# A chain of expert steps: scattered ids in buffers of their own, the weight split in wide pieces on ScalarE and VectorE alone, results scaled on ScalarE

## The chip, the cores and the metric

The kernel runs on one core of one Trainium2 chip. The metric is the device time of one execution in microseconds. Three runs of the kernel before took 517.78, 515.27 and 517.69 us, median 517.69. TensorE multiplies matrices, VectorE (DVE) and ScalarE (ACT) work element by element and can read PSUM, GpSimd (POOL) issues the indirect DMAs and can do elementwise work on SBUF, SyncE (SP) issues the other DMAs.

## The reference, cut to what matters

Three stages follow each other: a linear attention with decay over 2 x 768 tokens, a dense feed-forward block with layer norm, and a mixture of experts with sticky routing. The change touches the last stage alone:

```python
def _moe2_ref(x, w_gate, w_local, w1, w2):
    ...
    for b in range(B):
        prev_e = -1
        for s in range(S):
            fresh_e = int(np.argmax(logits[b, s]))
            if s == 0 or local_gate[b, s] < 0.5:
                e = fresh_e
            else:
                e = prev_e if prev_e >= 0 else fresh_e
            prev_e = e
            ...
            h = np.maximum(x[b, s] @ w1[e], 0.0)
            out[b, s] = p[e] * (h @ w2[e])
```

There are 8 experts, x has 384 columns, w1 is 384 x 1024 and w2 1024 x 384 per expert.

## The kernel before

All matmuls that need fp32 accuracy are made of products of two halves: a value is split into a high half (ScalarE writes it rounded, L143) and a low half (the rest, written by VectorE or POOL, L148), and three products are summed: high with high, high with low, low with high. Weights are split as well as activations.

The program up to about 318 us (attention, dense block, routing, and the first 256 rows of the fullest expert) is one list of tasks written out by hand (`ORDER`). Behind it stands the chain of expert steps, in an order that is also written by hand (`manual_schedule`). Each engine runs its instructions in the order in which the code issues them.

`step(e, t, before, o)` (L990) does the first half of tile t of expert e (128 rows each) and the second half of the tile that came before it:

- If t > 0, TensorE transposes the gathered rows of this tile (`xpose_pe`), and after the result (below) they are split into `xq` (`xpose_split`).
- The tile before: `turn_pe` transposes its hidden values `hs` (8 transposes), `result(o)` (L985) multiplies the finished output of the tile before that, which stands in PSUM bank 4, by its gate value `cur_p` into the buffer `o`, and POOL scatters `o` to the output rows `cur_i` by an indirect DMA. `turn_split` splits the transposed hidden values into `H`.
- `first` (L953) multiplies this tile by w1 in two halves of 512 columns, 9 matmuls each, and ScalarE writes each half through a Relu to `hs`.
- `second(before)` (L976) multiplies `H` by w2 into bank 4, 24 matmuls.
- In a step with t = 0 and e > 0 the weights are filled: w2 of this expert (needed in the next step's `second`) and w1 of the next expert. `fill` (L178) splits one piece of 512 columns; there are six of w2 (numbers 6 to 11) and six of w1 (0 to 5). `fl(0)` and `fl(1)` issue two and three pieces behind the two halves of `first`, `fl(2)` the rest behind `second`. `POOL_C` names four of the twelve pieces whose low half POOL writes; VectorE writes the others. The rows of the next expert's first tile are transposed and split in the same step, and POOL gathers rows for later tiles (`get`).
- `load_a`, `load_b` load raw weights for later experts on SP's queue.
- `shift` (L946) moves the ids and gate values along on VectorE with four copies: `cur_i`, `cur_p` get the next tile's, and `nxt_i`, `nxt_p` this tile's. The copy to `cur_i` has to wait until the scatter that reads `cur_i` is over.

`others(e, t)` (L1030) wraps every further tile of an expert into `tc.If` on the expert's count of rows; the steps for t = 1 to 11 are nested, so an expert with few rows jumps over the rest. At a jump each engine adds what it left out to its semaphore, so that others wait for it to be past the If. Which steps run depends on the data; with these inputs, by the trace, experts 2 and 4 have two further tiles, 5 and 6 have one, 0, 1, 3 and 7 have none.

The outputs go to `XR[t % 2]` for t > 0 and to `XH[e % 2]` for t = 0; `cur_i` and `cur_p` are one column each of two small tiles (`now`).

Of the kernel before, what the change touches and what calls it, by code (L numbers as in the profile page):

```python
# [14 lines left out]
I32 = mybir.dt.int32  # L15
ACTF = mybir.ActivationFunctionType
ALU = mybir.AluOpType
# [5 lines left out]
DM = NH * HD  # L23
# [3 lines left out]
NE, EF = 8, 1024  # L27
# [8 lines left out]
C_ID, C_MK, C_RV, C_FT, C_JT, C_IO, C_TI, C_EO, C_JH, C_NC = 0, 128, 192, 200, 204, 220, 348, 360, 361, 385  # L36
HMAX = 2 * JMAX
POOL_LO = (7, 9, 11)
POOL_C = (7, 9, 11, 2)


SEQ = [(0, 0), (0, 1), (0, 2), (0, 3), (1, 0), (0, 4), (0, 5), (1, 1), (1, 2), (1, 3), (1, 4), (1, 5)]
# [59 lines left out]
def moe_kernel(ctx: ExitStack, tc: tile.TileContext, rT, kT, rn, kn, vn, wt, un, gt, w_c, wg, w1, w2,  # L102
               cst, cst_b, out, dbg=None):
    nc = tc.nc
    PE, DVE, ACT, POOL, SP = nc.tensor, nc.vector, nc.scalar, nc.gpsimd, nc.sync
# [8 lines left out]
    B = [BB[:, i] for i in range(8)]  # L114
# [15 lines left out]
    XH = [const.tile([128, DM], F32, name=f"xh{i}") for i in range(2)]  # L130
# [11 lines left out]
    def split(dst_hi, dst_lo, src, relu=False, lo_eng=None):  # L142
        ACT.activation(out=dst_hi, in_=src, func=ACTF.Relu if relu else ACTF.Copy)  # L143
        if relu:
            DVE.scalar_tensor_tensor(out=dst_lo, in0=src, scalar=0.0, in1=dst_hi.bitcast(F32),
                                     op0=ALU.max, op1=ALU.subtract)
        else:
            (lo_eng or DVE).tensor_tensor(out=dst_lo, in0=src, in1=dst_hi.bitcast(F32), op=ALU.subtract)  # L148


    raws, sets = [], []

    XR = []

    def raw_set(pool, i):
        return pool.tile([128, KD, EF], F32, name=f"wa{i}"), pool.tile([128, KE, DM], F32, name=f"wb{i}")

    def split_set(pool, i):
        return tuple(pool.tile(s, F32R, name=f"{n}{i}") for n, s in (
            ("w1h", [128, KD, EF]), ("w1l", [128, KD, EF]), ("w2h", [128, KE, DM]), ("w2l", [128, KE, DM])))  # L160

    def load_a(e):
        if e < NE:
            for n in range(2):
                s = slice(n * 512, n * 512 + 512)
                SP.dma_start(out=raws[e % 2][0][:, :, s], in_=r3(w1[e], KD)[:, :, s])
# [11 lines left out]
    def fill(e, i, pool=POOL_LO):  # L178
        fill_set(raws[e % 2], sets[(e + 1) % 2], i, pool)

    def fill_set(raw, ws, i, pool=POOL_LO):
        a, c = raw
        w1h, w1l, w2h, w2l = ws
        if i < 6:
            k, n = i % 3, i // 3
            ns = slice(n * 512, n * 512 + 512)
            hi, lo, src = w1h[:, k, ns], w1l[:, k, ns], a[:, k, ns]
        else:
            n = slice((i - 6) * 512, (i - 5) * 512)
            hi, lo, src = (t.rearrange("p k f -> p (k f)")[:, n] for t in (w2h, w2l, c))  # L190
        split(hi, lo, src, lo_eng=POOL if i in pool else DVE)

    def gather(dst, off, n=NTOK):
        POOL.indirect_dma_start(dst, None, xd[0:n, :], IndirectOffsetOnAxis(ap=off, axis=0),
                                bounds_check=n - 1, oob_is_err=False)

    def xpose_pe(x, i):
        px = r3(B[6 + i][:, 0:DM], KD)
        for k in range(KD):
            PE.transpose(px[:, k, :], x[:, k * 128:(k + 1) * 128], ident)  # L200

    def xpose_split(i):
        s = slice(i * 128, i * 128 + 128)
        split(XQ[:, 0, :, s], XQ[:, 1, :, s], r3(B[6 + i][:, 0:DM], KD))

    if True:
# [496 lines left out]
        def load_top():  # L703
            a, c = raws[0]
            for t, w_ in ((a, w1), (c, w2)):
                POOL.indirect_dma_start(t.rearrange("p k f -> p (k f)"), None, w_.rearrange("e p f -> (e p) f"),
                                        IndirectOffsetOnAxis(ap=top_w, axis=0), bounds_check=128 * NE - 1, oob_is_err=False)
# [50 lines left out]

        now = []

        def load_early():
            ast.close()
            rst = ctx.enter_context(tc.tile_pool(name="cr", bufs=1, side="right", reuse_waits="tile"))
            raws.append(raw_set(rst, 0))
            sets.append(split_set(rst, 0))
            hs_.append(rst.tile([128, EF], F32, name="hs"))
            XE[0] = rst.tile([128, 2, DM], F32, name="xe0")
            load_top()
# [9 lines left out]
        def fill0(i):  # L778
            fill_set(raws[0], sets[0], i)
# [122 lines left out]
        def close():  # L902
            bst.close()
            cl = ctx.enter_context(tc.tile_pool(name="cl", bufs=1, reuse_waits="tile"))
            sets.append(split_set(cl, 1))
            raws.append(raw_set(cl, 1))
            XR.extend(x2)
            XP[1] = cl.tile([128, 2, DM], F32, name="xp1")
            now.extend(cl.tile([128, 2], t, name=f"now_{n}") for n, t in (("i", I32), ("p", F32)))

        def zX(i):
            POOL.memset((XE[0], XP[1])[i], 0.0)

        def rows(e, t):

            return XP[e % 2][:, t % 2] if t else XE[e % 2][:, 0]

        def get(e, t):
            if e < NE and t < JMAX:
                gather(rows(e, t), ids[:, e, t:t + 1])  # L920
# [13 lines left out]
        with tc.manual_schedule():  # L934
            for t in ORDER.split():
                name, *a = t.split(".")
                name, _, e = name.partition(":")
# [15 lines left out]
        def first(e, i, fl):  # L953

            w1h, w1l = sets[(e + 1) % 2][:2]
            xh, xl = XT[0]
            t = slice(128 * i, 128 * i + 128)
            for n in range(2):
                ns = slice(n * 512, n * 512 + 512)
                todo = [(a_, w_, k) for k in range(KD) for a_, w_ in ((xh, w1h), (xh, w1l))] + [(xl, w1h, k) for k in range(KD)]  # L960
                for q, (a_, w_, k) in enumerate(todo):
                    PE.matmul(out=B[n], lhsT=a_[:, k, t], rhs=w_[:, k, ns], start=(q == 0), stop=(q == 8))  # L962
                ACT.activation(out=hs[:, ns], in_=B[n], func=ACTF.Relu)  # L963
                fl(n)

        def turn_pe(n):
            pt = r3(B[2 + n], 4)
            for k in range(4):
                f = 4 * n + k
                PE.transpose(pt[:, k, :], hs[:, f * 128:(f + 1) * 128], ident)  # L970

        def turn_split(n):
            f = slice(4 * n, 4 * n + 4)
            split(hh[:, f, 0:128], hl[:, f, 0:128], r3(B[2 + n], 4))
# [7 lines left out]
                        PE.matmul(out=B[4][:, 0:DM], lhsT=a_[:, k, 0:128], rhs=w_[:, k, :], start=(q == 0), stop=(q == 23))  # L982
                        q += 1

        def result(o):  # L985
            DVE.tensor_scalar(out=o, in0=B[4][:, 0:DM], scalar1=cur_p, scalar2=None, op0=ALU.mult)  # L986
            POOL.indirect_dma_start(out[:, :], IndirectOffsetOnAxis(ap=cur_i, axis=0), o[:, :], None,  # L987
                                    bounds_check=NTOK - 1, oob_is_err=False)

        def step(e, t, before, o):  # L990

            if t:
                xpose_pe(rows(e, t), 1)
            if before is not None:
                for n in range(2):
                    turn_pe(n)
                result(o)
            if t:
                xpose_split(1)
                get(e, t + 1)  # L1000
            if before is not None:
                for n in range(2):
                    turn_split(n)

            todo = [] if t or e == 0 else [(e, q) for q in range(6, 12)] + [(e + 1, q) for q in range(6) if e + 1 < NE]
            parts = todo[:2], todo[2:5], todo[5:]

            def fl(n):
                for q in parts[n]:
                    fill(*q, POOL_C)  # L1010

            first(e, int(t > 0), fl)
            if t == 0 and e + 1 < NE:
                xpose_pe(rows(e + 1, 0), 0)
                xpose_split(0)
                get(e + 2, 0)
                get(e + 1, 1)
            if before is not None:

                if t + 1 < JMAX:  # L1020
                    tc.mark_branch_hint_location(f"end{e}.{t + 1}", nts[e] > 2 * t + 2, engines=[PE.engine])
                second(before)
            fl(2)
            if t == 0:
                load_a(e + 3)
                if e:
                    load_b(e + 2)
            shift(e, t)

        def others(e, t):  # L1030
            if t < JMAX:
                with tc.If(nts[e] > 2 * t, label=f"end{e}.{t}"):  # L1032
                    step(e, t, e, XR[t % 2])
                    others(e, t + 1)

        ctx.enter_context(tc.manual_schedule())
# [1 line left out]
        DVE.memset(now[1], 0.0)  # L1038
        ld_n(0)
        for e in range(NE):  # L1040
            step(e, 0, e - 1 if e else None, XH[e % 2])
            if e + 1 < NE:
                ld_n(e + 1)
            others(e, 1)
        for n in range(2):
            turn_pe(n)
        result(XH[0])
        for n in range(2):
            turn_split(n)
        second(NE - 1)  # L1050
        shift(None, 0)
        result(XH[1])


def layout(inputs):
# [70 lines left out]
```

## Time and profile before

| | |
|---|---|
| median of three runs | 517.69 us |
| the profiled execution | 517.72 us |
| its span, first to last instruction | 515.9 us |
| mean granted TensorE clock | 0.934 |
| TensorE busy | 405.6 us (79%) |
| VectorE busy | 333.3 us (65%) |
| ScalarE busy | 184.0 us (36%) |
| POOL busy | 223.3 us (43%) |

The span is shorter than the time by what lies around the first and the last instruction. In a profile, a row of a timeline gives the start, the duration, the engine, the source line, the operation, what it writes and reads, the shapes, how many like instructions were merged into the row, and in brackets how long the engine idled before it and what ended that. A source line can be that of a helper, as L143 and L148 here: there the tile names tell which split it is. The letter q behind an engine (DVEq) stands for its sequencer, which waits, branches and issues.

### The profile page before, as it was taken

The numbers are of one execution on the slowest core, as the hardware profiler recorded it, in microseconds if no ns is written. First come the engines' busy times: TensorE is split into PE (matmuls) and PEld (weight loads), VectorE is DVE, ScalarE is ACT, GpSimd is POOL, SyncE is SP. The second block draws the span as 40 slices with busy tenths as digits, with TensorE's granted clock in tenths as the row PEclk, the third lists the DMA queues.
The fourth block names the chain that finished last, engine by engine and source line by source line (L and its number), as shares of the span: only waits on it lengthen the run. The fifth ranks groups of instructions, "written<-read, shape, count | busy, mean of one in ns | idle before, by whom it ended". The sixth has DMA issues, their size and how long they took to land. (4 is left out here: it accounts for less than half of the span.)

```text
span 515.9 us, 8879 instructions
## 1 busy us (share of the span) xinstructions
PE 405.6 (79%) x3297; PEld 366.9 (71%) x3297; DVE 333.3 (65%) x685; ACT 184.0 (36%) x471; POOL 223.3 (43%) x212
## 2 busy tenths in 40 slices
PE   2447586999899799999999793596891979879675
PEld 2336575998799799889988673485881767768564
DVE  7998999758647857775785981736244543736341
ACT  1463453314135122212432541653251612707040
POOL 6879879264325412713041251635133432615141
PEclk9999799999899899999999996878996889989897
DMA  8863371051033050003309556075306270310000
GB/s 256 281 199 138 119 269 34 21 186 32 2 104 104 15 159 3 32 1 143 136 0 339 213 175 269 23 258 177 122 18 214 85 248 32 98 66 15 9 20 15
DMA packets 24848, 59.69 MB, mean 116 GB/s; under 512 B 3994, under 2 KB 10598, under 8 KB 24512
## 3 DMA queue, kind: packets, MB, share of 16 engines
q1 hardware_dynamic: 21856, 50.85, 29.0%
q0 software_dynamic: 2912, 7.88, 4.3%
q8 instruction: 38, 0.62, 0.5%
q14 instruction: 42, 0.34, 0.2%
HBM read 56.35 MB, written 5.70 MB: 120 GB/s over the span
## 5 line engine op out<-in xcount | busy, mean ns | idle before, releaser
L506 PE MATMUL banks<-wh,H 128*128 128x384 f32 x288 | 84.9, 356 | 7.6 <-DVE H L494 6.5
L962 PE MATMUL banks<-w1h,xq 128*128 128x512 f32 x168 | 64.6, 456 | 18.8 <-DVE xq L148 14.3
L148 POOL TENSOR_TENSOR w2l<-wb,w2h 128x512 fp32r<-128x512 f32 x27 | 35.0, 1304 | 63.2 <-ACT w2h L143 63.1
L506 PEld LDWEIGHTS banks<-wh,H 128*128 128x128 f32 x288 | 54.7, 196 | 9.8 <-DVE H L494 7.5
L962 PEld LDWEIGHTS banks<-w1h,xq 128*128 128x128 f32 x168 | 36.7, 221 | 30.0 <-DVE xq L148 16.0
L491 ACT ACTIVATE H<-banks 128x512 fp32r<-128x512 f32 x36 | 21.3, 594 | 80.3 <-PE banks L487 73.6
L506 PE MATMUL banks<-wl,H 128*128 128x384 f32 x144 | 49.9, 347 | 0.0
L982 PE MATMUL banks<-w2h,H 128*128 128x384 f32 x224 | 47.1, 343 | 0.0
L148 DVE TENSOR_TENSOR w1l<-wa,w1h 128x512 fp32r<-128x512 f32 x48 | 46.7, 1028 | 0.1
L487 PE MATMUL banks<-xq,wh 128*128 128x256 f32 x216 | 43.8, 301 | 0.4 <-DVE xq L470 0.4
L148 DVE TENSOR_TENSOR w2l<-wb,w2h 128x512 fp32r<-128x512 f32 x27 | 23.4, 868 | 30.4 <-ACT w2h L143 30.4
L970 PE MATMUL banks<-cs,hs 128*128 128x128 f32 x112 | 18.2, 317 | 29.1 <-DVEq L1032 21.0
L982 PEld LDWEIGHTS banks<-w2h,H 128*128 128x128 f32 x224 | 39.8, 192 | 1.0 <-ACT H L143 0.3
L963 ACT ACTIVATE hs<-banks 128x512 f32<-128x512 f32 x28 | 16.8, 598 | 58.5 <-PE banks L962 58.5
L970 PEld LDWEIGHTS banks<-cs,hs 128*128 128x128 f32 x112 | 15.1, 164 | 31.5 <-issue 31.5
L962 PE MATMUL banks<-w1l,xq 128*128 128x512 f32 x84 | 37.1, 441 | 0.0
L487 PEld LDWEIGHTS banks<-xq,wh 128*128 128x128 f32 x216 | 35.9, 202 | 1.1 <-DVE xq L470 0.6
L494 DVE SCALAR_TENSOR_TENSOR H<-banks,H 128x512 fp32r<-128x512 f32 x36 | 24.5, 684 | 18.7 <-ACT H L491 18.6
L987 POOL DMA_INDIRECT out<-xh,now_i x9 | 9.1, 1006 | 58.5 <-DVE xh L986 52.5
L143 ACT ACTIVATE H<-banks 128x512 fp32r<-128x512 f32 x28 | 15.6, 597 | 48.9 <-PE banks L970 48.9
L986 DVE TENSOR_SCALAR xh<-banks,now_p 128x384 f32<-128x384 f32 x9 | 5.6, 618 | 42.4 <-PEq L1032 22.1
L487 PE MATMUL banks<-xq,wl 128*128 128x256 f32 x108 | 31.9, 295 | 0.6 <-DVE wl L290 0.6
(234 smaller groups left out, 1055.2 us busy)
## 6 DMA issues: line engine op xcount, KB each, us to landing
wa<-in_w SPq DMA_DIRECT2D x16, 768.0 KB, 7.4
wb<-in_w SPq DMA_DIRECT2D x16, 768.0 KB, 10.3
wq<-in_w_c SPq DMA_DIRECT2D x12, 768.0 KB, 4.8
r<-in_rT SPq DMA_DIRECT2D x12, 256.0 KB, 3.9
k<-in_kT SPq DMA_DIRECT2D x12, 256.0 KB, 4.4
rn<-in_rn SPq DMA_DIRECT2D x12, 192.0 KB, 2.6
R<-in_vn SPq DMA_DIRECT2D x24, 96.0 KB, 2.6
kn<-in_kn SPq DMA_DIRECT2D x12, 192.0 KB, 3.9
```

The costliest lines, as they stand in the source:

```text
L143: ACT.activation(out=dst_hi, in_=src, func=ACTF.Relu if relu else ACTF.Copy)
L148: (lo_eng or DVE).tensor_tensor(out=dst_lo, in0=src, in1=dst_hi.bitcast(F32), op=ALU.subtract)
L487: PE.matmul(out=ph[:, i, :], lhsT=a, rhs=x_[:, k, :], start=(q == 0), stop=(q == 8))
L491: ACT.activation(out=hh[:, ring(n)], in_=r3(B[3 + n % 2], 2), func=ACTF.Relu)
L494: DVE.scalar_tensor_tensor(out=hl[:, ring(n)], in0=r3(B[3 + n % 2], 2), scalar=0.0, in1=hh[:, ring(n)].bitcast(F32), op0=ALU.max, op1=ALU. ...
L506: PE.matmul(out=bank_o(b, g), lhsT=a[:, f2, s][:, i], rhs=w_[:, 2 * p + i, DM:], start=(p + i + n == 0), stop=(p == NP - 1 and i == 1 and ...
L962: PE.matmul(out=B[n], lhsT=a_[:, k, t], rhs=w_[:, k, ns], start=(q == 0), stop=(q == 8))
L963: ACT.activation(out=hs[:, ns], in_=B[n], func=ACTF.Relu)
L970: PE.transpose(pt[:, k, :], hs[:, f * 128:(f + 1) * 128], ident)
L982: PE.matmul(out=B[4][:, 0:DM], lhsT=a_[:, k, 0:128], rhs=w_[:, k, :], start=(q == 0), stop=(q == 23))
L986: DVE.tensor_scalar(out=o, in0=B[4][:, 0:DM], scalar1=cur_p, scalar2=None, op0=ALU.mult)
L987: POOL.indirect_dma_start(out[:, :], IndirectOffsetOnAxis(ap=cur_i, axis=0), o[:, :], None, bounds_check=NTOK - 1, oob_is_err=False)
```

## The change

Three things change, all in the chain of expert steps. The pieces of a fill in the chain are 1024 columns wide, three of w1 and three of w2, and VectorE writes all low halves (`fill2`; the fills that `ORDER` issues stay as they are). `result` runs on ScalarE. Each of the four output buffers gets an id buffer of its own, into which VectorE copies `cur_i`; the scatter reads that copy.

```diff
-POOL_C = (7, 9, 11, 2)
...
+    def fill2(e, i):
+
+        a, c = raws[e % 2]
+        w1h, w1l, w2h, w2l = sets[(e + 1) % 2]
+        if i < 3:
+            split(w1h[:, i], w1l[:, i], a[:, i])
+        else:
+            n = slice((i - 3) * 1024, (i - 2) * 1024)
+            split(*(t.rearrange("p k f -> p (k f)")[:, n] for t in (w2h, w2l, c)))
...
+        XO = []
...
+            XO.extend(zip((*XR, *XH), (cl.tile([128, 1], I32, name=f"oi{n}") for n in range(4))))
...
-        def result(o):
-            DVE.tensor_scalar(out=o, in0=B[4][:, 0:DM], scalar1=cur_p, scalar2=None, op0=ALU.mult)
-            POOL.indirect_dma_start(out[:, :], IndirectOffsetOnAxis(ap=cur_i, axis=0), o[:, :], None,
+        def result(n):
+            o, oi = XO[n]
+            DVE.tensor_copy(out=oi, in_=cur_i)
+            ACT.activation(out=o, in_=B[4][:, 0:DM], func=ACTF.Copy, scale=cur_p)
+            POOL.indirect_dma_start(out[:, :], IndirectOffsetOnAxis(ap=oi[:, 0:1], axis=0), o[:, :], None,
                                     bounds_check=NTOK - 1, oob_is_err=False)
...
-            todo = [] if t or e == 0 else [(e, q) for q in range(6, 12)] + [(e + 1, q) for q in range(6) if e + 1 < NE]
-            parts = todo[:2], todo[2:5], todo[5:]
+            todo = [] if t or e == 0 else [(e, q) for q in range(3, 6)] + [(e + 1, q) for q in range(3) if e + 1 < NE]
+            parts = todo[:1], todo[1:3], todo[3:]
...
             def fl(n):
                 for q in parts[n]:
-                    fill(*q, POOL_C)
+                    fill2(*q)
...
-                    step(e, t, e, XR[t % 2])
+                    step(e, t, e, t % 2)
...
-            step(e, 0, e - 1 if e else None, XH[e % 2])
+            step(e, 0, e - 1 if e else None, 2 + e % 2)
...
-        result(XH[0])
+        result(2)
...
-        result(XH[1])
+        result(3)
```

## Rows read from the trace of the kernel before

**Rows 1.** Waits from 316 us on: who, for whom: total us, times, longest.

```profile
PE banks L970 <- DVEq L1032: 21.0, 3, 11.7
DVE now_i L947 <- DMA out<-x,now_i: 20.3, 4, 7.8
PE banks L962 <- DVE xq L148: 14.3, 4, 3.7
```

**Rows 2.** Timeline of expert 3's first step, ScalarE, VectorE, POOL, TensorE: start, us.

```profile
380.36 1.14 ACT L143 ACTIVATE w2h<-wb 128x512 fp32r<-128x512 f32 x2
381.96 0.60 ACT L963 ACTIVATE hs<-banks 128x512 f32<-128x512 f32 x1 [0.46 <-PE banks L962]
...
384.15 1.38 DVE L148 TENSOR_TENSOR w2l<-wb,w2h 128x512 fp32r<-128x512 f32 x1 [0.35 <-ACT w2h L143]
...
385.12 1.33 POOL L194 DMA_INDIRECT x<-xd,ids  x1
385.46 0.54 DVE L148 TENSOR_TENSOR xq<-banks,xq 128x384 fp32r<-128x384 f32 x1
385.50 0.86 PE L982 MATMUL banks<-w2h,H 128*128 128x384 f32 x4
385.92 5.84 DVE L148 TENSOR_TENSOR w1l<-wa,w1h 128x512 fp32r<-128x512 f32 x5
...
388.11 1.28 POOL L148 TENSOR_TENSOR w2l<-wb,w2h 128x512 fp32r<-128x512 f32 x1
...
391.68 0.14 DVE L947 COPY now_i<-now_i 128x1 int32<-128x1 int32 x1
```

**Rows 3.** Timelines at the Ifs behind experts 1, 3 and 7.

```profile
336.39 0.62 DVE L986 TENSOR_SCALAR xh<-banks,now_p 128x384 f32<-128x384 f32 x1 [0.98 <-DVEq L1032]
...
398.04 0.62 DVE L986 TENSOR_SCALAR xh<-banks,now_p 128x384 f32<-128x384 f32 x1 [5.97 <-DVEq L1032]
...
502.60 0.62 DVE L986 TENSOR_SCALAR xh<-banks,now_p 128x384 f32<-128x384 f32 x1 [2.91 <-DVEq L1032]
```

**Rows 4.** Timelines at the start of expert 2's second tile: ScalarE, VectorE, TensorE.

```profile
350.49 0.47 ACT L143 ACTIVATE xq<-banks 128x384 fp32r<-128x384 f32 x1
...
354.16 0.14 DVE L947 COPY now_i<-now_i 128x1 int32<-128x1 int32 x1
...
356.06 1.28 DVE L148 TENSOR_TENSOR H<-banks,H 128x512 fp32r<-128x512 f32 x2
356.19 2.07 PE L962 MATMUL banks<-w1h,xq 128*128 128x512 f32 x4 [3.52 <-DVE xq L148]
```

**Rows 5.** Source lines of the splits: count, ns min/median/max, first to last us, shape.

```profile
L148 DVE TENSOR_TENSOR w1l<-wa,w1h x48: 669/682/3611, 252.3 to 478.5; 128x512 fp32r<-128x512 f32 x48
...
L290 DVE TENSOR_TENSOR wl<-d,wh x5: 953/958/2039, 37.3 to 96.7; 128x768 fp32r<-128x768 f32 x5
...
L143 ACT ACTIVATE w1h<-wa x54: 613/623/634, 251.5 to 474.7; 128x512 fp32r<-128x512 f32 x54
...
L287 ACT ACTIVATE wh<-d x12: 828/843/848, 15.4 to 95.8; 128x768 fp32r<-128x768 f32 x12
```

**Rows 6.** Windows: busy us (count) of PE, PEld, DVE, ACT, POOL, clock, DMA.

```profile
356.20:359.30 3.10, 3.10 (x7) 2.47 (x8) 1.14 (x2) 0.60 (x1) 1.81 (x2) 0.51 0.90 300
359.30:360.50 1.20, 1.20 (x7) 0.96 (x6) 0.00 (x0) 0.00 (x0) 0.00 (x0) 1.00 1.04 329
...
350.00:352.70 2.70, 1.68 (x7) 1.05 (x6) 2.70 (x2) 1.94 (x5) 2.67 (x3) 1.00 0.12 42
```

**Rows 7.** Timeline of VectorE and TensorE at the start of expert 2's third tile.

```profile
365.11 0.15 DVE L947 COPY now_i<-now_i 128x1 int32<-128x1 int32 x1 [7.77 <-DMA out<-x,now_i]
...
366.25 0.55 PE L200 MATMUL banks<-cs,x 128*128 128x128 f32 x3 [1.44 <-DMA x<-xd,ids]
```

**Rows 8.** Timeline of VectorE at the end of expert 7's fill.

```profile
499.29 0.14 DVE L947 COPY now_i<-now_i 128x1 int32<-128x1 int32 x1
```

**Rows 9.** DMA queues of the page: packets, MB, share of 16 engines.

```profile
q14 instruction: 42, 0.34, 0.2%
```

## The prediction

> **What bounds the kernel now.** The change touches the last third of the program alone, the chain of expert steps from about 318 us to the end, so I read only that. First the waits of that stretch [rows 1]: TensorE waits longest for the sequencer of VectorE at the If of L1032 (21.0 us, 3 times), and another 14.3 us, 4 times, for the low half of xq that VectorE writes. VectorE in its turn waits 20.3 us, 4 times, for scatters that still read now_i. So the first question is whether VectorE is late because it is busy or because it waits for the scatters.
>
> The timeline answers it. In the first step of expert 3 [rows 2] VectorE writes eight lower halves of 512 columns, POOL the other four. Alone, one takes VectorE 0.68 us. But the VectorE piece that meets a POOL piece takes 1.38 us, and five pieces of w1l take 5.84 us where about 3.1 would do: while POOL runs its two pieces (from 388.11, 1.28 us each) VectorE stands. The shift that ends the step starts at 391.68, although TensorE has been done since 386.4 [rows 2]. This is the bound: the fill on VectorE, in six steps (experts 1 to 6).
>
> What follows a fill differs. If the expert has no second tile (experts 1, 3), TensorE begins the next step when VectorE is past the If [rows 3]. If it has one (experts 2, 4, 5, 6), VectorE still has to write the result and then xq's low half, and TensorE, which has run six of its 18 matmuls on the high half, starts again 2.03 us after the shift [rows 4]. The 20.3 us of scatter waits are in steps with t=1: there the shift waits up to 7.8 us [rows 1], but in that longest case TensorE waits for the gathered rows until 366.25, 1.44 us, and not for the shift at 365.1 [rows 7]. Nothing on the path hangs on that shift.
>
> **The change part by part.** The sum is made against the profiled execution's 517.72 us (span 515.9, 1.8 around it); the median of the runs, 517.69, is the same.
>
> *Pieces of 1024, VectorE alone.* No 1024-wide split is in the trace. VectorE: 0.68 us for 512, 0.96 for 768 without POOL beside it, so 0.27 per 256 and 1.23 for 1024; back to back, pieces of 512 start 0.60 apart (two H splits of that width take 1.28 us together [rows 4]), so 1.15 for 1024. ScalarE: 0.62 and 0.84, so 1.06, and starts 0.96 apart (0.52, as two take 1.14 together [rows 2], plus two times 0.22) [rows 5]. Now the step of expert 3 again [rows 2]. ScalarE's first w2 piece starts at 380.36 as before; the second hs is set by TensorE, 381.96; the next two w2 pieces start at 382.46 and 383.42. VectorE writes their lower halves from 383.55 and 384.70, xq from 385.85 (was 385.46), then w1 from 386.31, 387.46, 388.61, and the shift starts at 389.76. That is 1.92 us before 391.68, and it is still VectorE that ends the step: ScalarE's last piece, by the same spacing, ends at 387.7, TensorE at 386.4. For experts 1 and 3 the whole 1.92 reaches the path: 3.8 us. Expert 7 splits w2 alone; there the third wide piece ends the fill and the shift starts some 0.4 us after 499.29 [rows 8].
>
> *What POOL loses.* Its gathers come about 3 us sooner in the step. They run beside VectorE without harm: under the gather from 385.12 (1.33 us), xq's half took 0.54 us [rows 2]. Here a rule of the Trainium skill speaks against the row: "SBUF — State Buffer", section "SBUF: two separate sides", has a GpSimd operation that reads SBUF and a VectorE operation with two SBUF inputs shut each other out for the whole instruction. For the POOL pieces the rows agree (5.84 us above). For gathers, which read their ids from SBUF, they don't; by the rule's words the sum would be that of the slow rival below.
>
> *The result on ScalarE.* The nearest row is xq's high half, also 384 columns out of PSUM, 0.47 us, against 0.62 on VectorE [rows 3, 4]. In a step with t=0 it lies beside the eight transposes and costs nothing; without that cover it would cost 0.47. In a step with t=1 it costs more than its length: ScalarE runs in order, and behind the result stand xq's high half, H's high half and hs. The result needs now_p, which the shift writes after the fill. Before, xq's high half was written at 350.49, long ahead of the shift at 354.16 [rows 4]. After, the order from the shift's start is two copies (0.21), result 0.48, xq high 0.48, hand-over 0.06: TensorE starts 1.23 after the shift, 0.80 sooner than the 2.03 of today, but with 18 matmuls to do, not 12. Today these six take 1.68 us, at a granted clock of 1.00, the level of 2.4 GHz; at 0.51, near that of 1.2 GHz, seven take 3.10, so 2.7 for six [rows 6]. After the restart the clock is 0.51 for 3.1 us and then 1.00 [rows 6]; 18 matmuls outlast that, so the added ones run at the high level and I take 1.8, near the lower end. A step with t=1 after a fill so gets 1.92 + 0.80 - 1.8 = 0.9 (from 0 to 1.0), four times: 3.7 us.
>
> *Own buffers of scattered ids.* Worth nothing by itself: the shift that waited is late for nobody [rows 7], and the copy of the ids (0.15) is beside the result. In the steps with t=2 TensorE waits for the gather, whose issue comes forward with the step and whose loads ahead of it are issued about 1 us sooner; I let the gain pass through. The price if it doesn't is 1 us in two steps.
>
> *The last result* is 0.13 us shorter. Chain: 3.8 + 3.7 - 0.4 + 0.1 = 7.2 us.
>
> *The far jump.* Where an expert has no second tile, each engine jumps over eleven nested steps. After experts 1, 3 and 7 TensorE waits for VectorE at that jump. The three jumps are alike in the source, yet VectorE idles 0.98, 5.97 and 2.91 us over them [rows 3]. The page has 42 packets of an instruction queue with 0.34 MB, 8 KB each [rows 9]: I read the two long ones as code that wasn't there yet. Against 0.98 they cost 4.99 and 1.93, 6.9 us, all on the path. The change draws these places anew, since the count of VectorE's instructions alters in every step; and less of VectorE's code lies between the branch and its target, as the wait for the scatter in front of the shift falls away in each nested step. I take one chance in five per jump, an estimate below the two in three seen. The likeliest case is then that none of the three stalls: 6.9 us more. Bounds: all of it, or 5.0 lost at expert 1 as well. "Runtime: NRT & Kernel Launch", section "Instruction fetch mechanics", of the Trainium skill says that a taken branch to code outside the two blocks held stalls for a fetch; by that, with blocks of the trace's size, a jump as short as one block never stalls, and the sum would be the forecast.
>
> Forecast: 517.7 - 7.2 - 6.9 = 503.6 us.
>
> **The rivals.**
> The stalls stay, at these jumps or at others of the same price. For it: two of three have one today, and the code on ScalarE grows. Time: 517.7 - 7.2 = 510.5. If only one is left: 505.5 (the short one) to 508.6 (the long one).
>
> Slower: the gathers lock VectorE out as the POOL pieces did. Place: the two gathers of 1.33 us per filling step, which now fall on wide w2 pieces. A step then ends 0.74 us later than today rather than 1.92 sooner. Price: 2 x 2.66 + 4 x 2.66 = 16 us off the gain of 7.2; with the jumps as today 526.5, with all stalls gone 519.6. With the jumps as today it decides against the change once a gather costs VectorE more than 0.6 us (7.2 us over some twelve gathers). Against it stands xq's 0.54 us under a gather [rows 2].
>
> The change does little: ScalarE's order takes back in steps with t=1 what the fill gains. If the six matmuls run at the low clock and the gather eats the rest, the chain is worth 3.8 - 0.3 = 3.5 us, 514.2 with the stalls in place.
>
> **How the numbers follow.** No stall left, 503.6: 0.50. One stall left, 505.5 to 508.6: 0.25. Stalls as today, 510.5: 0.13. Little gained, 512 to 516: 0.07. Slower, 519 to 527: 0.05. The range takes in the first three, widened by the bounds of the steps with t=1 (0.4 us more gain, 3.6 less) and by the gathers' 2 us: 500.5 to 512. A measurement of this kernel tells 0.5%, 2.6 us, from no change; faster than that (under 515.1) 0.90, within it 0.05, slower 0.05.
>
> **What would show it right or wrong.** VectorE's w1l pieces: three of about 1.23 us, none over 1.4; a longest piece of 2.5 would be the lock-out. The shift of expert 3 some 9.4 us after ScalarE's first w2 piece, not 11.3 [rows 2]. The first ScalarE operation after a shift in t=1 is the result, and TensorE starts about 1.2 us behind the shift with 18 matmuls. The waits of TensorE for VectorE at L1032 fall from 21 us to under 10; if one of them is still above 6, a jump stalls. The row of DMA waits in front of the shift is gone, and the steps with t=2 don't move by it. What would make it wrong: stalls moved to TensorE's or ScalarE's code, or the gather landing no sooner.

## The result, and the profile after

The changed kernel took 499.98 us (median of four runs, 499.33 to 506.58), the kernel before 516.48 beside it; the ratio is 0.971, 95% interval 0.963 to 0.979. On the 517.72 us of the profiled execution this is 502.7, where 503.6 was forecast. By the two medians the ratio is 0.968, which gives 501.2: the 506.58 weighs on the first figure. That slowest run is the profiled execution (span 504.8), so its sum has to be read with care. Against the profile before, 2.3 us of it lie ahead of the chain, where nothing was changed. There TensorE's granted clock fell, in a stretch in which it stayed at 1.00 before:

Windows of the changed kernel, columns as in [rows 6]:

```profile
288.00:291.00 3.00, 1.72 (x13) 1.51 (x14) 2.93 (x10) 1.54 (x4) 1.15 (x1) 0.98 1.00 389
291.00:294.00 3.00, 2.73 (x17) 2.43 (x17) 2.18 (x7) 0.60 (x1) 0.00 (x0) 0.50 0.08 31
```

The chain alone is the better measure: from the first of the eight transposes of expert 1's first step to the end of the span it took 197.4 us before (318.45 to 515.9) and takes 184.1 now (320.74 to 504.8), 13.4 less. The sum had said 14.1.

The waits of the changed kernel from 312 us on, which answer to [rows 1]:

```profile
PE banks L974 <- ACT xq L142: 13.7, 4, 3.4
PE banks L982 <- DVEq L1046: 12.3, 3, 4.7
PE banks L209 <- DMA x<-xd,ids: 6.0, 3, 2.6
```

The wait at the If went from 21.0 to 12.3 us, longest 4.7 instead of 11.7. The wait for xq's low half on VectorE became one for its high half on ScalarE, and is as long as before, 13.7 for 14.3. The wait of VectorE for scatters is gone; what that is worth alone is run e3 below.

The first step of expert 3, timeline of the changed kernel, which answers to [rows 2] and the second line of [rows 3]:

```profile
380.15 2.00 ACT L142 ACTIVATE w2h<-wb 128x1024 fp32r<-128x1024 f32 x2
...
381.24 2.36 DVE L147 TENSOR_TENSOR w2l<-wb,w2h 128x1024 fp32r<-128x1024 f32 x2 [0.88 <-ACT w2h L142]
...
383.52 0.55 DVE L147 TENSOR_TENSOR xq<-banks,xq 128x384 fp32r<-128x384 f32 x1
383.98 3.49 DVE L147 TENSOR_TENSOR w1l<-wa,w1h 128x1024 fp32r<-128x1024 f32 x3
...
387.39 0.15 DVE L959 COPY now_i<-now_i 128x1 int32<-128x1 int32 x1
...
388.74 1.94 PE L982 MATMUL banks<-cs,hs 128*128 128x128 f32 x8 [4.68 <-DVEq L1046]
```

The three wide pieces of w1l take 3.49 us where five of 512 took 5.84; ScalarE's first w2 piece began at 378.05, the shift comes 9.34 us later, not 11.32. TensorE now waits 4.68 us there, not 11.66: 1.98 from the shift, the other 5.0 from the jump.

The wide splits over the whole chain, by source line (columns as in [rows 5]):

```profile
L147 DVE TENSOR_TENSOR w2l<-wb,w2h x21: 1218/1224/1227, 327.6 to 486.9; 128x1024 fp32r<-128x1024 f32 x21
...
L147 DVE TENSOR_TENSOR w1l<-wa,w1h x18: 1215/1218/1222, 332.4 to 465.6; 128x1024 fp32r<-128x1024 f32 x18
...
L142 ACT ACTIVATE w1h<-wa x18: 1048/1056/1062, 330.8 to 463.7; 128x1024 fp32r<-128x1024 f32 x18
```

Not one of 39 pieces on VectorE is longer than 1.227 us; the estimates were 1.23 and 1.06. This says little on gathers: without POOL's pieces the gathers of a filling step mostly come before the first wide piece (in expert 3's, from 376.06 and 377.39, the first piece at 379.13), and only two of the 39 meet one. The trace before can tell. There pieces of w1l, 512 wide, ran under gathers; timeline of the kernel before, POOL and VectorE:

```profile
386.75 1.34 POOL L194 DMA_INDIRECT x<-xd,ids  x1 [0.31 <-PEq L1032]
...
387.13 0.69 DVE L148 TENSOR_TENSOR w1l<-wa,w1h 128x512 fp32r<-128x512 f32 x1
```

A piece that lies wholly under a gather took 0.69 us, where 0.68 is the median [rows 5].

The second tiles of experts 2 and 5, timeline of the changed kernel, which answers to [rows 4]; the bracket is TensorE's wait:

```profile
352.52 0.15 DVE L959 COPY now_i<-now_i 128x1 int32<-128x1 int32 x1
...
352.81 0.58 ACT L1000 ACTIVATE x<-banks,now_p 128x384 f32<-128x384 f32 x1 [2.31 <-issue]
353.29 0.48 ACT L142 ACTIVATE xq<-banks 128x384 fp32r<-128x384 f32 x1
...
353.82 0.50 PE L974 MATMUL banks<-w1h,xq 128*128 128x512 f32 x1 [3.42 <-ACT xq L142]
...
442.93 0.50 PE L974 MATMUL banks<-w1h,xq 128*128 128x512 f32 x1 [3.43 <-ACT xq L142]
```

Two windows behind these restarts, columns as in [rows 6]:

```profile
353.80:356.80 3.00, 2.98 (x13) 2.43 (x14) 2.24 (x8) 1.45 (x3) 2.05 (x2) 1.00 0.90 307
...
444.90:447.90 3.00, 3.00 (x9) 2.35 (x8) 0.25 (x3) 0.60 (x1) 1.03 (x1) 0.50 0.13 42
```

TensorE starts 1.30 us after the shift, with all 18 matmuls to do. In expert 2 the granted clock stayed at 1.00, the level of 2.4 GHz, and they took 4.48 us; in expert 5, after the same wait, it was still 1.00 until 444.4, 1.5 us behind the restart, then fell to 0.50, that of 1.2 GHz, and they took 6.01.

The jump behind expert 7, timeline of the changed kernel, and under it the DMA view of its stretch from 488 to 491 us:

```profile
488.26 0.14 DVE L963 COPY now_p<-tab 128x1 f32<-128x1 f32 x1
...
491.22 1.06 PE L982 MATMUL banks<-cs,hs 128*128 128x128 f32 x8 [3.01 <-DVEq L1046]
491.23 0.15 DVE L999 COPY oi<-now_i 128x1 int32<-128x1 int32 x1 [2.83 <-DVEq L1046]
```

```profile
DMA packets 1, 0.01 MB, mean 3 GB/s; under 512 B 0, under 2 KB 0, under 8 KB 0
## 3 DMA queue, kind: packets, MB, share of 16 engines
q14 instruction: 1, 0.01, 0.8%
```

One stall is left: VectorE idles 2.83 us at a jump that takes it 0.6 elsewhere. From 488.45 to 491.1 us no engine of the core runs, and one packet of the instruction queue is all that moves.

Where the 13.4 us of the chain lie, by the time from the first transpose of one step to that of the next (T1 is the first further tile of an expert, T2 the second; the tail goes to the end of POOL's last scatter; the numbers are worked out from the starts in the timelines). The other columns are the experiments of the next section; e11 is the changed kernel with one useless instruction more.

| from ... to | before | after | e1 wide | e4 no POOL | e5 result back | e6 split first | e11 pad | e12 |
|---|---|---|---|---|---|---|---|---|
| expert 1 | 17.90 | 16.40 | 16.82 | 16.32 | 16.38 | 16.68 | 15.91 | 16.35 |
| expert 2 | 12.63 | 12.24 | 12.45 | 12.25 | 12.20 | 12.38 | 11.93 | 12.21 |
| expert 2 T1 | 17.65 | 14.94 | 14.15 | 14.95 | 14.85 | 13.41 | 14.26 | 11.99 |
| expert 2 T2 | 9.99 | 10.00 | 9.99 | 10.00 | 10.00 | 9.99 | 10.00 | 9.99 |
| expert 3 | 21.41 | 14.44 | 14.43 | 18.42 | 14.42 | 14.43 | 14.42 | 14.43 |
| expert 4 | 12.52 | 12.04 | 12.52 | 11.79 | 12.08 | 11.28 | 12.22 | 11.50 |
| expert 4 T1 | 16.78 | 16.14 | 14.20 | 14.06 | 14.29 | 13.80 | 14.50 | 11.91 |
| expert 4 T2 | 9.99 | 11.62 | 9.99 | 9.99 | 10.00 | 9.99 | 10.00 | 9.99 |
| expert 5 T1 | 16.56 | 15.19 | 14.62 | 12.99 | 14.68 | 12.28 | 13.64 | 12.28 |
| expert 6 T1 | 16.71 | 15.18 | 14.53 | 12.98 | 14.74 | 12.29 | 13.66 | 12.35 |
| expert 7 | 12.12 | 12.44 | 10.16 | 9.87 | 10.16 | 12.68 | 10.16 | 10.16 |
| tail | 8.88 | 9.10 | 7.72 | 7.73 | 7.72 | 10.15 | 7.70 | 7.68 |

(The first steps of experts 5 and 6 take 9.9 to 10.0 us everywhere and are left out.)

### The profile page after: what moved, and what is told of

Read it like the earlier page. It is cut to its first block, busy times and chain, and to the rows that moved or that the text cites. A ratio compares the mean times of both kernels' runs of the same rounds, so it can differ in the third digit from the quotient of the medians.

```text
span 504.8 us, 8805 instructions
## 1 busy us (share of the span) xinstructions
PE 405.7 (80%) x3297; PEld 369.1 (73%) x3297; DVE 318.5 (63%) x673; ACT 189.0 (37%) x447; POOL 185.0 (37%) x185
## 5 line engine op out<-in xcount | busy, mean ns | idle before, releaser
L974 PE MATMUL banks<-w1h,xq 128*128 128x512 f32 x168 | 62.2, 439 | 14.3 <-ACT xq L142 13.7
L500 ACT ACTIVATE H<-banks 128x512 fp32r<-128x512 f32 x36 | 21.3, 594 | 80.3 <-PE banks L496 73.6
L147 DVE TENSOR_TENSOR H<-banks,H 128x512 fp32r<-128x512 f32 x28 | 18.3, 687 | 47.1 <-ACT H L142 47.1
L147 DVE TENSOR_TENSOR w2l<-wb,w2h 128x1024 fp32r<-128x1024 f32 (+1 forms) x27 | 29.2, 1104 | 25.8 <-ACT w2h L142 24.9
L1001 POOL DMA_INDIRECT out<-xh,oi x9 | 9.1, 1012 | 79.3 <-ACT xh L1000 73.0
L982 PE MATMUL banks<-cs,hs 128*128 128x128 f32 x112 | 18.0, 314 | 20.8 <-DVEq L1046 12.3
L147 DVE TENSOR_TENSOR w1l<-wa,w1h 128x512 fp32r<-128x512 f32 (+1 forms) x36 | 32.4, 951 | 0.1
L982 PEld LDWEIGHTS banks<-cs,hs 128*128 128x128 f32 x112 | 14.9, 162 | 23.0 <-issue 23.0
L496 PE MATMUL banks<-xul,wh 128*128 128x256 f32 x108 | 30.6, 284 | 1.1 <-DVE xul L479 1.1
L496 PE MATMUL banks<-xuh,wh 128*128 128x256 f32 x108 | 31.3, 290 | 0.0
```

The lines of the kernel that those rows point to most:

```text
L496: PE.matmul(out=ph[:, i, :], lhsT=a, rhs=x_[:, k, :], start=(q == 0), stop=(q == 8))
L500: ACT.activation(out=hh[:, ring(n)], in_=r3(B[3 + n % 2], 2), func=ACTF.Relu)
L1001: POOL.indirect_dma_start(out[:, :], IndirectOffsetOnAxis(ap=oi[:, 0:1], axis=0), o[:, :], None, bounds_check=NTOK - 1, oob_is_err=False)
```

## The experiments

All times are medians beside runs of the kernel before on the same chip (516.62 to 515.11 us), with the ratio's 95% interval.

**e1, wide pieces alone.**

```diff
 (the kernel before, with fill2, todo and parts of the change)
...
-                    fill(*q, POOL_C)
+                    fill2(*q)
```

> Only the fill of the chain is changed: pieces of 1024 columns, low halves on VectorE alone; result stays on VectorE, the scatter reads now_i as before. Theory (POOL's pieces lock VectorE out): the shift of every filling step starts 1.9 us sooner after the turn's start than before (15.06 us in expert 3's first step becomes 13.1), TensorE in steps with t=1 still restarts 2.0 us after the shift with 12 matmuls, so six filling steps give 1.9 each, 11 us, and the jumps come on top: 506 us with the stalls of before, 499 with none. Rival (the gain is the jumps alone): the shift moves by under 0.5 us and the time stays at 511 or above.

493.4 us, ratio 0.957 (0.951 to 0.964): 22 us, more than the whole change gives. Expert 3's shift comes 13.09 us after its first transpose, 15.07 before, as the theory has it, and no jump stalled. For that case 499 was expected, so 5.6 us more came than the theory gives. The waits from 312 us on:

```profile
PE banks L980 <- DVEq L1042: 10.1, 3, 4.7
PE banks L972 <- DVE xq L148: 7.9, 4, 2.0
```

The steps with T1 gain 1.9 to 3.5 us where the shift gives 2.0 to 2.2. In experts 2 and 4, with 3.5 and 2.6, the rest is the wait for the gathered rows of T2: 1.44 and 0.62 us before, none here. TensorE's wait for xq's low half falls from 3.6 to 2.0 us on the mean, but the twelve matmuls behind it took 4.2 to 4.6 us, little less than before (4.4 to 4.6).

**e2, result on ScalarE alone.**

```diff
-            DVE.tensor_scalar(out=o, in0=B[4][:, 0:DM], scalar1=cur_p, scalar2=None, op0=ALU.mult)
+            ACT.activation(out=o, in_=B[4][:, 0:DM], func=ACTF.Copy, scale=cur_p)
```

> Only result is moved to ScalarE; fills in pieces of 512 with POOL, scatter reads now_i. Theory: nothing in steps with t=0; in the four steps with t=1 after a fill TensorE restarts 1.3 us after the shift, not 2.0, but with 18 matmuls. If the six added ones cost 1.4 to 1.8 us (TensorE at 1.2 GHz after its idle time) each such step loses 0.7 to 1.0 us, 3 to 4 us in all: 519 to 521 us. Rival (restart at 2.4 GHz as in experts 2 and 4 of the changed kernel, where the six cost under 0.1 us): each gains 0.7, 513.7 us. Stalls at the jumps may add or take up to 7 us; they are read apart in the profile.

512.61 us, ratio 0.995 (0.991 to 0.999), where 519 to 521 was expected. The steps with T1 became longer, as the theory has it, but by 0.28, 0.09, 0.98 and 0.93 us. The small gain comes from elsewhere: expert 3's jump, where TensorE waited 11.66 us, now costs 6.65, though VectorE does there what it did; it has one instruction less in each step. In expert 2's T1:

```profile
353.37 0.58 ACT L986 ACTIVATE x<-banks,now_p 128x384 f32<-128x384 f32 x1 [3.84 <-issue]
353.85 0.48 ACT L143 ACTIVATE xq<-banks 128x384 fp32r<-128x384 f32 x1
...
354.38 0.80 PE L962 MATMUL banks<-w1h,xq 128*128 128x512 f32 x1 [5.42 <-ACT xq L143]
```

The high half of xq stands behind the result in ScalarE's queue, the result waits for now_p, and TensorE has nothing to do for 5.42 us.

**e3, id buffers alone.** (The scatter reads a copy of cur_i, all else as before.)

> Only the id buffers are added: VectorE copies cur_i and the scatter reads the copy; result stays on VectorE, fills as before. Theory: the scatter waits in front of the shift (20.3 us of VectorE) go away and no step of TensorE moves by over 0.3 us, so 516.5 us but for what the jumps do, as VectorE's code grows by the copies. Rival (the shift that waited did hold the path): the steps with t=2 start sooner by 1 us each, 514.

515.81 us, ratio 1.001 (0.997 to 1.005). The waits for scatters in front of the shift are gone and the time is the same, with the stalls behind experts 3 and 7 still there (VectorE idles 6.90 and 2.82 us): the id buffers are worth nothing by themselves.

**e4, pieces of 512, but none on POOL.**

```diff
-POOL_C = (7, 9, 11, 2)
+POOL_C = ()
```

> Fills stay in pieces of 512, but no piece of the chain is POOL's: VectorE writes all twelve. Theory (lock-out, not width): five pieces of w1l no longer take 5.84 us but six take some 3.7, the shift of a filling step comes 1.5 to 1.9 us sooner after the turn's start, 9 to 11 us in all before the jumps: 506 to 508 us with the stalls of before. Rival (width decides): VectorE's two more pieces per step of w1 and w2 cost what the lock-out cost, the shift moves by under 0.5 us, 515 us or above.

492.73 us, ratio 0.955 (0.949 to 0.962), where 506 to 508 was expected. This line alone gives what the wide pieces give; what counts is that POOL keeps away, not the width. Timeline of expert 3's first step and the second tile of expert 5, then a window behind that restart:

```profile
379.88 3.69 DVE L148 TENSOR_TENSOR w1l<-wa,w1h 128x512 fp32r<-128x512 f32 x6
...
388.92 1.30 PE L970 MATMUL banks<-cs,hs 128*128 128x128 f32 x5 [8.67 <-DVEq L1032]
...
439.81 1.20 PE L962 MATMUL banks<-w1h,xq 128*128 128x512 f32 x4 [1.44 <-DVE xq L148]
```

```profile
439.80:442.90 3.10, 3.09 (x14) 2.54 (x15) 1.15 (x2) 0.60 (x1) 1.82 (x2) 1.00 0.15 43
```

Six pieces of w1l take 3.69 us, where five took 5.84 with POOL beside them. Behind a wait of 1.44 us, instead of 3.5, TensorE's clock stays at 1.00, where it was 0.51 before [rows 6], and the twelve matmuls take 3.1 us instead of 4.6; so the steps with T1 of experts 5 and 6 get 3.6 to 3.7 us shorter where the shift comes only 2.1 sooner. Over the four steps the clock gives 5.8 us that the expectation had not. And this kernel still pays 4 us at the jump behind expert 3.

**e5, the changed kernel with result back on VectorE.** (The line of e2, undone; wide pieces and id buffers stay.)

> The changed kernel with result back on VectorE; wide pieces and id buffers stay. Theory (result on ScalarE, ahead of xq's high half, costs time in the four steps with t=1): these steps take 14.2 to 14.6 us from turn to turn as with the wide pieces alone, not 14.9 to 16.1, and the step after them stays at 10.0 where the changed kernel had 11.6 once; 494 us, 6 us under the changed kernel's 500. Rival (the id buffers and their copies cost it, or the jumps do): 498 us or above, and the steps with t=1 stay at 14.9 or above.

495.23 us, ratio 0.958 (0.955 to 0.961), 4.8 us under the changed kernel. The time is as expected, the reason is not. In the profiles 3.7 of it are the jump behind expert 7 and the tail (12.44 and 9.10 became 10.16 and 7.72); the steps with T1 at 14.3 to 14.9 are no shorter than those of e11 (13.6 to 14.5), which has result on ScalarE and in whose profile the clock stayed at 1.00 behind all four waits. So what result on ScalarE costs a step was not shown here; its place in the queue is the next run.

**e6, the split of xq ahead of result.**

```diff
-                result(o)
             if t:
                 xpose_split(1)
+            if before is not None:
+                result(o)
+            if t:
                 get(e, t + 1)
```

> The changed kernel with one change of order: in steps with t=1 and more, xq is split ahead of result, so ScalarE writes xq's high half without waiting for now_p, and VectorE writes the low half without a result in front. Theory (the wait of ScalarE's queue for now_p is the cost): TensorE does six matmuls ahead of the shift again and restarts 1.5 us after it, 0.5 sooner than with result on VectorE; the steps with t=1 take 13.5 to 14 us, 492 us. Rival (ScalarE's order does not matter, the restart is bound by the shift alone): 499 to 500.

493.55 us (four runs from 490.0 to 498.9), ratio 0.950 (0.945 to 0.954). Timeline of expert 6's second tile:

```profile
454.31 0.49 ACT L142 ACTIVATE xq<-banks 128x384 fp32r<-128x384 f32 x1
...
456.44 0.14 DVE L959 COPY now_i<-now_i 128x1 int32<-128x1 int32 x1
...
456.68 0.58 ACT L1000 ACTIVATE x<-banks,now_p 128x384 f32<-128x384 f32 x1 [1.88 <-DVE now_p L960]
...
457.77 1.21 PE L974 MATMUL banks<-w1h,xq 128*128 128x512 f32 x4 [1.26 <-DVE oi L999]
```

ScalarE still waits for now_p, but nothing that TensorE needs soon stands behind. TensorE does six matmuls ahead of the shift and waits 1.26 us, not 3.4; the steps take 12.3 where no gather is late. The stall behind expert 7 is still in this kernel (12.68, and 10.15 in the tail).

**e7 and e8, a prefetch hint for VectorE at the jumps,** in the changed kernel and in the kernel before.

```diff
-... engines=[PE.engine])
+... engines=[PE.engine, DVE.engine])
```

> The changed kernel; VectorE too gets the prefetch hint that TensorE already has, ahead of the branch of each jump. Theory (VectorE's stall of 2.7 us at the jump behind expert 7 is code that is not there): the wait of TensorE at that jump falls from 3.0 to 0.7 us, its clock stays up in the tail (9.1 becomes 7.7), 496 to 497 us. Rival (VectorE waits there for another engine, or the hint comes too late): 500, the wait unchanged.

> The kernel before with nothing but the prefetch hint for VectorE at the jumps. Theory (the long waits at the jumps behind experts 3 and 7 are code that is not there): VectorE idles 1.0 us over the jump behind expert 3, not 5.97, and 1.0, not 2.91, behind expert 7; 6.9 us and some clock in the tail, 508 to 510 us. Rival (the waits are for a semaphore of another engine): 516, both as before.

The kernel before: 506.43 us, ratio 0.979 (0.976 to 0.982). TensorE's wait behind expert 3 went from 11.66 to 6.69, that behind expert 7 from 2.70 to 0.36, the tail from 8.88 to 7.71:

```profile
387.77 1.94 PE L970 MATMUL banks<-cs,hs 128*128 128x128 f32 x8 [6.69 <-DVEq L1032]
387.80 0.62 DVE L986 TENSOR_SCALAR xh<-banks,now_p 128x384 f32<-128x384 f32 x1 [1.02 <-DVEq L1032]
```

The theory's numbers came in, but the hint adds instructions to every step of VectorE as well, so this run alone doesn't tell the hint from a new place of the code. The changed kernel: 500.61 us, no gain, where 496 to 497 was expected. The stall behind expert 7 is gone (3.01 to 0.76 us), but one behind expert 3 has come:

```profile
389.44 1.94 PE L982 MATMUL banks<-cs,hs 128*128 128x128 f32 x8 [8.58 <-DVEq L1046]
389.46 0.15 DVE L999 COPY oi<-now_i 128x1 int32<-128x1 int32 x1 [4.88 <-DVEq L1046]
```

**e9 and e10, the gather first, and hints.** As e6, with get ahead of result, and the hint of TensorE at expert 0's jump too (e9); with a hint of VectorE right ahead of shift (e10).

```diff
             if t:
                 xpose_split(1)
+                get(e, t + 1)
             if before is not None:
                 result(o)
-            if t:
-                get(e, t + 1)
```

> As the run with the split ahead of result, and two things more: in steps with t=1 and more the gather of the next tile's rows is issued ahead of result's scatter (and so ahead of the weight loads), and TensorE gets its prefetch hint for the jump behind expert 0 too. Theory (the steps with t=2 wait for a gather queued behind 3 MB of loads; the 6.2 us of TensorE at the jump behind expert 0 are code that is not there): the gaps of 1.6 and 2.1 us ahead of the steps with t=2 fall to 0.6 or less, the gap behind expert 0 falls from 6.2 to under 3 us; 6 us in all, 487 to 488 us, 484 if no jump of VectorE stalls. Rival (the gather is late whatever its place, POOL being blocked by the scatter before): gaps as they were, 490 to 494.

> As the run with the gather first, and VectorE gets the prefetch hint as well, right ahead of shift. Theory: the code for the jumps behind experts 3 and 7 is fetched while VectorE still writes low halves or waits, so no jump costs VectorE over 1.2 us and the gaps of TensorE behind experts 1, 3 and 7 are 4.7, 4.7 and 0.7 us: 484 us. Rival (the hint stands too close to the branch to help, or a fetch behind the weight loads comes late anyway): a stall of 2 to 4 us at one jump or more, 486 to 490.

e9: 487.29 us, ratio 0.944 (0.941 to 0.946). The waits for gathered rows ahead of the steps with T2, 1.20 and 1.67 us in e6, are gone. TensorE's wait behind expert 0 stayed, 6.7 us, so the hint did nothing there, and what holds it is open. Behind expert 7 it still stalls (3.04 us). e10: 487.89 us, its rival's case; the stall behind expert 7 went (0.76), one behind expert 3 came:

```profile
385.21 1.94 PE L982 MATMUL banks<-cs,hs 128*128 128x128 f32 x8 [9.61 <-DVEq L1048]
385.24 0.15 DVE L999 COPY oi<-now_i 128x1 int32<-128x1 int32 x1 [5.91 <-DVEq L1048]
```

The DMA view of its stretch from 379.5 to 385.1 us:

```profile
DMA packets 569, 1.14 MB, mean 203 GB/s; under 512 B 16, under 2 KB 16, under 8 KB 568
## 3 DMA queue, kind: packets, MB, share of 16 engines
q1 hardware_dynamic: 568, 1.13, 73.6%
q14 instruction: 1, 0.01, 0.3%
```

The one packet of code stands among 568 of the weight loads that have just been issued. Behind expert 7 there are no loads, and a stall comes with 2.8 to 3.1 us of idle time; behind expert 3 there are, and it comes with 4.9 to 6.9. The packet of code starts 1.95 us ahead of TensorE's restart in both cases, so the longer stall is longer before the packet moves; that it waits behind the loads there fits, and no run tried it. A hint did not keep expert 3's away in e7 and e10.

**e11 and e12, one useless instruction.** The copy to the id buffer is issued twice, in the changed kernel and in e9.

```diff
             DVE.tensor_copy(out=oi, in_=cur_i)
+            DVE.tensor_copy(out=oi, in_=cur_i)
```

> The changed kernel with the copy of cur_i to the id buffer issued twice, one useless VectorE instruction of 0.15 us per step: nothing is taken off any engine, only VectorE's code grows to the length it has in the run with result back on VectorE. Theory (whether a jump stalls hangs on where VectorE's code happens to lie): the jump behind expert 7 no longer stalls, as there; TensorE's gap in front of the tail falls from 3.0 to 0.7 us, its clock stays up in the tail (9.1 becomes 7.7), and the steps with t=1 stay at 15 to 16 us: 496 to 497 us. Rival (the stall of the changed kernel has to do with result on ScalarE): gap 3.0 and 500 us or a little more.

> The run with the gather first, with the same useless second copy. Theory: no jump of VectorE stalls, TensorE's gaps behind experts 1, 3 and 7 are 4.7, 4.7 and 0.7 us, the rest as in that run: 485 us, 2.3 us under it. Rival: a stall turns up at another jump, 487 to 490.

e11: 495.96 us, ratio 0.964 (0.960 to 0.968), 4.0 us under the changed kernel for more work (2.7 us when each median is taken against the kernel before beside it). The jump and the tail are 3.7 us of it in the profiles. The steps with T1 did not stay at 15 to 16 us, as was expected: this profile is the fastest run (490.92), TensorE waits 3.43 us in them as in the changed kernel, but its clock stayed at 1.00 in all four. e12: 484.36 us, ratio 0.940 (0.936 to 0.944), the best of all, 31 us under the kernel before. Behind expert 7 in e11, where 3.01 and 2.83 stood:

```profile
476.96 1.07 PE L982 MATMUL banks<-cs,hs 128*128 128x128 f32 x8 [0.73 <-DVEq L1047]
476.97 0.15 DVE L999 COPY oi<-now_i 128x1 int32<-128x1 int32 x1 [0.56 <-DVEq L1047]
```

So a stall comes or goes with one instruction that does nothing; I take it that it hangs on where VectorE's code happens to lie, as the instruction moves all code behind it. That it is a fetch of code is borne out by all the traces: in each of the eleven stalls of the fourteen kernels a packet of the instruction queue starts 1.9 to 2.1 us ahead of TensorE's restart, and at the 23 jumps behind experts 1 and 3 without a stall none starts in the last 4.6 us. Behind expert 7 one can start in the last 2 us without a stall (1.54 us in e11); the trace doesn't say whose code a packet holds.

## Why the prediction was right or wrong, point by point

**The bound was right.** VectorE locked out by POOL's pieces: e4 shows it alone, e1 together with the width. For POOL's pieces the page "SBUF — State Buffer" of the Trainium skill, section "SBUF: two separate sides", agrees with the runs (5.84 us for five, 3.69 for six). For gathers the prediction set that rule aside by xq's 0.54 us, and this row can't do it: the rule, as the prediction gives it, is for two SBUF inputs, and xq's split reads PSUM and one tile in SBUF. The w1l piece of 0.69 us under a gather reads two, and it bears the prediction out. The slow rival fell for another reason as well: the gathers hardly meet the wide pieces.

**Experts 1 and 3.** 1.92 us each were forecast; the shifts came 1.50 and 1.98 sooner, and the steps behind them gained 0.39 and 0.48 more, as TensorE had idled less and its clock came up sooner, which the sum had not: 4.4 us for 3.8.

**Steps with T1.** The time of the restart was right (1.30 us after the shift; 1.23 was said, and the result took 0.58, not 0.48). The term that was mis-sized is "18 matmuls outlast that, so the added ones run at the high level and I take 1.8". It took for granted that the clock falls behind the wait as before. In experts 2 and 4 it did not, and 18 matmuls took as long as 12 had (4.48 against 4.45 us); in 5 and 6 it fell late, and the six cost 1.4. So the steps of experts 2, 5 and 6 gained 2.71, 1.38 and 1.53 instead of 0.9. In expert 4 the gather that T2 needs did not come forward with the step, which the prediction let pass: TensorE waited 2.63 us for it, not 0.62, the clock fell in T2, and T1 and T2 together lost 1.0 where expert 2's gained 2.7. The price named for such a gather was 1 us; here it was 3.7. With the gather issued ahead of the result no step waits for it (e9). In sum 4.6 for 3.7: a cheaper restart and a dearer gather, two misses of opposite sign.

**Expert 7 and the last result.** The shift came 0.39 later, as said (0.4). The tail is 0.22 longer, not 0.1 shorter. TensorE had waited 3.01 us in front of it and ran 3.4 us of it at the low clock, as before behind 2.70 us; the low stretch began 1.0 us later in the step, which fits the difference. Without a stall the tail is 7.72 with result on VectorE (e1) and 7.70 with it on ScalarE (e11), so the gain of 0.1 is not seen.

**The jumps.** The likeliest case, no stall, did not come; the one-stall rival did: 5.0 of 6.9 us. The step that failed is what was made of "less of VectorE's code lies between the branch and its target": that a shorter jump stalls less, and, drawn from the Trainium skill's "Runtime: NRT & Kernel Launch", section "Instruction fetch mechanics", that a jump as short as one block of the trace's size never stalls. What the section says, that a taken branch to code not held waits for a fetch, agrees with the lone packet at expert 7. But the length of the jump doesn't decide: in e1 the steps jumped over are those of the kernel before, unchanged, and none of the three jumps stalls, while the changed kernel with its shorter ones stalls behind expert 7. Of the 42 jumps behind experts 1, 3 and 7 in the fourteen kernels profiled here, eleven stall, none of them behind expert 1. So one chance in five per jump was about right, but nine of the fourteen kernels have a stall, and that none is left was not the likelier case.

**The sum.** In the profiles 13.4 us of the chain for 14.1: 4.4 for 3.8, 4.6 for 3.7, -0.4 for -0.4, -0.2 for 0.1, and 5.0 for 6.9. That it came so close is in part luck: the steps gave 1.5 us more than forecast, and the stall that stayed took 1.9 back. Nor do the ends of the range, 500.5 and 512, follow from the widths named for them: 510.5 and 3.6 us less gain alone make 514.1.

**Id buffers** are worth nothing by themselves (e3), as said.

**What the forecast did not see** is that the parts don't add up. The fill alone gives 493.4 us, the whole change 499.98. Of the 6.6 us between them some 4 are the stall that one more instruction takes away (e11 against the changed kernel, 3.7 in the profiles). The rest is near what e11 and e5 differ by, against the kernel before beside each (0.964 and 0.958, some 3 us): result is on ScalarE in one and on VectorE in the other. It fits the wait of 3.4 us that result's place in ScalarE's queue makes in every step with T1, where e1's is 2.0, and e6 shows that its order alone takes the wait to 1.3. But the profiled steps don't show it: in e1 and e11 they take the same time to 1 us, as the clock held in e11. By the sum's own terms a forecast for the fill without result would have shown this: 1.9 us for each such step against 0.9.

**What stays open:** why the other runs of the changed kernel lie some 6.6 us under the profiled one. Its gather at expert 4, its clock in T1 and the stretch ahead of the chain are 3.3, 3.1 and up to 5.9 us over what e11 or other profiles show, which is enough, but those runs have no trace.

## What to carry to other kernels

Before VectorE's work is shared with POOL, compare its longest instruction beside POOL's with its shortest; here five pieces beside two of POOL's took longer than six alone, and the sharing cost more than it took over. On an engine that runs in order, put an instruction that waits for a late value behind those that don't. And where engines jump over code, read the idle time at each jump apart: an edit that only adds a useless instruction moved the time by 3 to 4 us here, so an edit is judged by the stretches between the jumps, not by the total.

## What the runs showed of the hardware that was not expected

A jump of the same source left VectorE idle for 0.6 to 1.0 us or for 2.8 to 6.9; each long wait had a packet of code 1.9 to 2.1 us ahead of its end, and was longer where weight loads were in flight. TensorE's clock may hold or fall behind one and the same wait of 3.4 us (18 matmuls in 4.48 or 6.01 us; it held in two steps of four in the changed kernel and in all four of e11), and held behind 1.44. A gather beside pieces of 512 on VectorE took 1.31 to 1.34 us on POOL in the trace before, 1.03 apart from them, while the pieces stayed at 0.67 to 0.69. And the stretch ahead of the chain, in which no run changed more than the jump behind expert 0, ended between 314.8 and 320.7 us; a difference of a few microseconds between two single executions says nothing of a change in the chain.
